# Output weights in three whole-row transfers, and the first chunk's output groups in two passes

## The chip, the core and the metric

The kernel runs on one core of a Trainium2 chip. The metric is the device time of one execution in microseconds. A time without a profile is the median of several runs; a profiled execution has a time of its own. In the profile PE is TensorE (PEld its weight loads), DVE is VectorE, ACT is ScalarE, POOL is GpSimd and SP is SyncE. A trailing q (SPq, POOLq) means that the engine only issues a transfer. L531 is line 531 of the kernel.

## What is computed

Cosine attention over 8 batches of 12 heads, 448 positions and 64 dimensions, then two matrix products with a leaky ReLU between them:

```python
q_n = q / (norm(q) + 1e-6);  k_n = k / (norm(k) + 1e-6)
scores = q_n @ k_n.T / 0.1
attn = exp(scores - max) / (sum + 1e-9)
x = (attn @ v).transpose(0, 2, 1, 3).reshape(3584, 768)
h = x @ w_in                        # 768 x 2048
out = maximum(0.01 * h, h) @ w_out  # 2048 x 768, result float32
```

## The kernel before

**Attention.** Heads are handled in pairs: slot s is one pair, or one half of a pair of pairs from slot 12 on, 48 slots in all. Each slot goes through a row of steps, each a small function. `load_qk(s)` reads float32 rows on SP's queue (L150 from slot 12 on, L158 to L161 before). `squares(s)` runs on POOL (L216, L224), `sums(s)` adds them up on DVE (L232, L238), `roots(s)` takes logarithm and exponential on ACT (L245, L246), and `normalise(s)` multiplies on DVE (L253, L254, then L260 or L270, which writes `qn`). `transposes(s)` is done by PE below slot 12 (L284) with a copy out of PSUM by DVE (L325); from slot 12 on it is a DVE transpose (L306), and for odd slots six transfers on SP's queue carry the result into `qkT` (L315). `scores` is PE work (L346) followed by exponentials on ACT (L355). `attend(j)` makes the row sums and the products with v on PE (L366), the reciprocal on ACT (L377, L378) and the scaling on DVE (L397), which writes `xT`, the input of the first product. `settle(s)` is normalise, transposes (from slot 12 on), `hold` and the squares of slot s + 2. `hold` (L616, POOL) and `hold_loads` (L613, SP) are tiny operations that read `qn`, so that what is queued behind them on their engine starts no sooner.

**The two products.** The 3584 tokens go in eight chunks of 384 or 512. `first(c, m)` makes one of 16 row blocks of the hidden layer for chunk c: PE (L494) and an activation on ACT (L505) into `hT`. `second(c, ts, half)` makes 128 tokens by 384 output columns: 16 matmuls, one for each row block m (L531), a copy by DVE from PSUM into `osb` (L541), and after the second half a store on SP's queue (L548). Chunk 0 makes all three `ts` of the left half and then all three of the right half; the others make both halves of a `ts` in turn.

**Order.** The program order on each engine is written out by hand up to slot 15. There `feed_groups(0, n)` puts the next n pieces of chunk 0's work between attention steps. A planner spreads the later chunks over 42 visits, and chunk 7 comes last.

**PSUM.** There are eight banks. `banks(1)` or `banks(2)` deals out the bank, or the aligned pair, that was dealt longest ago. PE's next use of a bank waits until ACT or DVE has read out what was there before.

**Weights.** `w_in` comes in four transfers on POOL's queue (L104), `w_out` in two (L110): each brings half of the columns of all 16 row blocks, casting float32 to bf16, so one contiguous piece is 384 columns (768 bytes as written) and a transfer has 128 x 16 of them. The first is issued in the last of the six opening slots, the second after `squares(10)` and one load of v. Loads of v (L176, L184) are on the same queue.

The code writes the hand order with s = 6, so its `s + 7` is slot 13.

Of the kernel before, what the change touches and what calls it, by code (L numbers as in the profile page):

```python
# [8 lines left out]
F32 = mybir.dt.float32  # L9
BF16 = mybir.dt.bfloat16  # L10
AF = mybir.ActivationFunctionType
ALU = mybir.AluOpType
# [4 lines left out]
def kernel(  # L17
# [10 lines left out]
    nc = tc.nc  # L28
    B, H, S, D = q.shape
    N_tok, D_model = out.shape  # L30
# [4 lines left out]
    MAIN = 3 * 128  # L35
# [5 lines left out]
    MT = D_ff // 128  # L41
# [33 lines left out]
    def banks(count, keep=None):  # L75
        lo, hi = (0, 8) if not deals["apart"] else (0, 4) if count == 2 else (4, 8)
        x = min(
            (i for i in range(lo, hi, count) if not set(range(i, i + count)) & set(kept.values())),
            key=lambda i: max(age[i : i + count]),
        )  # L80
        deals["n"] += 1
        age[x : x + count] = [deals["n"]] * count
        if keep:
            kept[keep] = x
        return ps[:, x] if count == 1 else ps[:, x : x + count]
# [19 lines left out]
            out=w_in_sb[:, e::2, n0 : n0 + D_ff // 2], in_=w_in_r[e, :, :, n0 : n0 + D_ff // 2]  # L105
        )

    def load_w_out(half):
        n0 = half * HALF
        gp.dma_start(out=w_out_sb[:, :, n0 : n0 + HALF], in_=w_out_r[:, :, n0 : n0 + HALF])  # L110

    def main(x, b, h0, nh):
        return x[b, h0 : h0 + nh, 0:MAIN].rearrange("h (p t) d -> p h t d", t=3)
# [57 lines left out]
    def load_v(j):  # L171
        if j >= B * NQ:
            return
        b, jj = divmod(j, NQ)
        vb[j] = vbp.tile([128, 4, 3, D], BF16, name="v_b")
        gp.dma_start(out=vb[j], in_=main(v, b, 4 * jj, 4))  # L176
# [32 lines left out]
    def squares(s, eng=gp, parts=(0, 1)):  # L209
        if s >= NSLOT:  # L210
            return
        sq = sqt[s % 3]
        if s >= OLD:
            sqs[s] = sq
            x = raw[s].rearrange("p (t d) -> p t d", d=D)
            gp.tensor_tensor(sq[:, :, :D], x, x, op=ALU.mult)  # L216
            return
        sqs[s] = halves(sq.rearrange("p t d -> p (t d)"), D + 1)
        for i in parts:
            x, y = raw[s][i], sqs[s][i]  # L220
            if eng is nc.scalar:
                nc.scalar.activation(y[..., :D], x, func=AF.Square)
            else:
                eng.tensor_tensor(y[..., :D], x, x, op=ALU.mult)  # L224

    def sums(s, parts=(0, 1)):
        if s >= NSLOT:
            return
        if s not in ss:
            ss[s] = smp.tile([128, 14], F32, name="ss")  # L230
        if s >= OLD:
            nc.vector.tensor_reduce(  # L232
                ss[s], sqs[s], axis=AX.X, op=ALU.add
            )
            return
        for i in parts:
            o = ss[s][:, 0:8] if i == 0 else ss[s][:, 8:14]
            nc.vector.tensor_reduce(  # L238
                o.rearrange("p (h t) -> p h t", h=2), sqs[s][i], axis=AX.X, op=ALU.add
            )  # L240
# [239 lines left out]
    def chunk_cols(c):  # L480
        return (0, MAIN) if c % 2 == 0 else (MAIN, 512)
# [41 lines left out]
    def second(c, ts, half):  # L523
        c0, n = chunk_cols(c)
        last = c == B - 1 and ts == n // 128 - 1
        pieces = ((0, HALF // 2), (HALF // 2, HALF)) if last and half == 1 else ((0, HALF),)
        x, end = c0 + ts * 128, c0 + (ts + 1) * 128
        for lo, hi in pieces:
            po2 = banks(1)
            for m in range(MT):  # L530
                nc.tensor.matmul(  # L531
                    out=po2[:, : hi - lo],
                    lhsT=hT[c][:, m, ts * 128 : (ts + 1) * 128],
                    rhs=w_out_sb[:, m, half * HALF + lo : half * HALF + hi],
                    start=(m == 0), stop=(m == MT - 1),
                )
            if half == 0 or last:
                osb[c, ts] = osp.tile([128, D_model], F32, name="osb")
            o = osb[c, ts]
            cols = slice(half * HALF + lo, half * HALF + hi)  # L540
            nc.vector.tensor_copy(out=o[:, cols], in_=po2[:, : hi - lo])  # L541
            if half == 1 or last:
                if not last:
                    cols = slice(0, D_model)
                row = 0
                while row < 128:
                    dst, cnt = rows_of(c, x + row, end)
                    nc.sync.dma_start(out=dst[:, cols], in_=o[row : row + cnt, cols])  # L548
                    row += cnt


    work = {}
    for c in range(B):
        c0, n = chunk_cols(c)
        groups = [(KT * n, lambda c=c, m=m: first(c, m)) for m in range(MT)]
        order = [(ts, half) for half in range(2) for ts in range(n // 128)] if c == 0 else [
            (ts, half) for ts in range(n // 128) for half in range(2)
        ]
        work[c] = groups + [
            (MT * HALF, lambda c=c, ts=ts, half=half: second(c, ts, half)) for ts, half in order  # L560
        ]

    def feed_groups(c, count):
        for _ in range(count):
            work[c].pop(0)[1]()
# [49 lines left out]
    def hold(x):  # L615
        gp.tensor_copy(out=seen, in_=x)  # L616
# [35 lines left out]
    for s in range(NPAIR):  # L652
        j = s // 2 - 1 if s >= 2 else None
        even = s % 2 == 0
        n = s + 2 if 0 < s < NPAIR - 2 else None
        last = s == NPAIR - 1
        if not last:
            scores(s, (0,))
        scores(s, (1,))
        if j is not None and not even:  # L660
            products(j, 1)
        if j is not None and even:
            totals(j)
        elif not last:
            fill(2)
        if n and s > 1:
            sums(n, (0,))
        if not last:
            normalise(s + 1)
        if s < 2:  # L670
            sums(s + 2, (0, 1) if s == 0 else (0,))
        if s == 0:
            load_qk(7)
        elif s in (2, 3):
            hold_loads(s + 1)
            load_qk(s + 6)
        if s == 3:
            sums(n, (1,))
        if late:
            scale(late.pop(), 1)  # L680
        if j is not None and not even:
            scale(j, 0)
        if last:
            scale(j, 1)
            sums(NPAIR)
            sums(NPAIR + 1)
            load_w_out(0)
        else:
            hold(qn[s + 1][:, 6, 0, 0:1])
        squares(s + 3)  # L690
        if s == 0:
            load_v_rem(0, range(2, 4))
        if s in (1, 2):
            load_v(s)
        if last:
            load_v(NQ)
            load_v_rem(1)
        elif s < 2:
            load_w_in(s)
        elif s > 2:  # L700
            load_w_in(s - 1)
        if n and even:
            sums(n, (1,))
        scores(s, (2,))
        if last:
            for m in range(2):
                first(0, m, (0, 2))
            scores(s, (3,))
            for kt in (1, 3):
                for m in range(2):  # L710
                    first(0, m, (kt,))
        elif not even:
            fill(2)
            if s == 3:
                roots(n)
            transposes(s + 1)
            scores(s, (3,))
            if s == 1:
                sums(n, (1,))
                roots(n)  # L720
            fill(2)
        elif s == 0:
            roots(2)
            transposes(1)
            fill(2)
        else:
            transposes(s + 1)
            products(j, 0)
            if s == NPAIR - 2:
                scores(s + 1, (0,))  # L730
            if n:
                roots(n)
        if j is not None and not even and not last:
            late.append(j)
# [39 lines left out]
    hold(qn[s + 2][:, 6, 0, 0:1])  # L774
    squares(s + 4)
    load_v(s // 2 + 1)
    load_w_out(1)
    sums(s + 3)
    feed_groups(0, 2)
    scores(s + 1, (0, 1))  # L780
# [12 lines left out]
    normalise(s + 4)  # L793
    hold(qn[s + 4][:, 6, 0, 0:1])
    squares(s + 5)
    load_v(s // 2 + 2)
    hold_loads(s + 4)
    load_qk(s + 7)
# [6 lines left out]
    def settle(s, more=()):  # L805
        normalise(s)
        if s >= OLD:
            transposes(s)
        hold(qn[s][:, 6, 0, 0:1])
        for x in (*more, s + 2):  # L810
            squares(x)
# [9 lines left out]
    settle(s + 5, (s + 6,))  # L821
    hold_loads(s + 5)
    load_qk(s + 8)
    feed_groups(0, 1)
    sums(s + 6)
    transposes(s + 5)
    attend(NQ)
# [3 lines left out]
    scores(s + 3, (3,))  # L831
    load_qk(s + 9)
    settle(s + 6)
    sums(s + 7)
    feed_groups(0, 1)
    roots(s + 7)

    scores(s + 4, (2,))
    scores(s + 5, (0, 1))
    feed_groups(0, 1)  # L840
    attend(NQ + 1)
    load_qk(s + 10)
    settle(s + 7)
    sums(s + 8)

    scores(s + 5, (2, 3))
    feed_groups(0, 1)
    load_vq(0)
    roots(s + 8)
    load_qk(s + 11)  # L850
    settle(s + 8)
    load_qk(s + 12)
    sums(s + 9)
    feed_groups(0, 1)
    roots(s + 9)
    attend(NEWQ - 1)
    feed_groups(0, 1)

# [131 lines left out]
```

## Time and profile before

| | |
|---|---|
| median of three runs | 417.78 us (417.63 to 418.49) |
| profiled execution | 416.43 us |
| its span in the trace | 414.6 us |
| PE busy | 407.1 us, 98% of the span |
| DVE, ACT, POOL busy | 221.5, 250.2, 114.6 us |
| granted PE clock | 1.00 in every stretch |
| first and second `w_out` transfer | issued at 29.11 and 49.12 us, landed 23.2 and 21.3 us later |
| chunk 0's output groups on PE | between 55.00 and 80.89 us |
| DMA packets of POOL's queue, q0 | 15488, 11.80 MB |

The profiled execution's time is 1.83 us more than its span. Times in the trace count from the start of the span. A row of the timeline gives start, duration, engine, line, operation, and in brackets idle time before it with what ended it. The DMA rows give, for a queue and a stretch, its packets, megabytes and the time that its packets took as a share of 16 DMA engines; shares of the two queues can add up to more than 100%, because packets in flight overlap.

### The profile page before, as it was taken

How to read it: one execution, taken by the hardware profiler on the slowest of the kernel's cores; microseconds unless marked ns; L12 is line 12 of the kernel's file. 1: busy time of each engine (PE TensorE's matmuls, PEld its weight loads, DVE VectorE, ACT ScalarE, POOL GpSimd, SP SyncE). 2: the span in 40 equal slices, each digit the busy share in tenths (PEclk: the TensorE clock that was granted, in tenths of full speed). 3: DMA queues.
4: the chain of work that ended last, by engine and by line, in shares of the span. 5: the costliest groups of instructions: out<-in, count | busy, mean ns of one | idle time of the engine just before them, and what ended most of it. 6: DMA issues, size and time to landing. Idle time of an engine off the chain costs nothing.

```text
span 414.6 us, 11342 instructions
## 1 busy us (share of the span) xinstructions
PE 407.1 (98%) x4799; PEld 212.3 (51%) x4799; DVE 221.5 (53%) x387; ACT 250.2 (60%) x431; POOL 114.6 (28%) x149
## 2 busy tenths in 40 slices
PE   8899999999999999999999999999999999999997
PEld 3335555544555555544455555554445555654565
DVE  6977976855778556766474964464621301210022
ACT  5997876378657785668865688547764464004300
POOL 4875543433234132413331433122210000000000
PEclk9999999999999999999999999999999999999999
DMA  7999998775377851884275681742442100020022
GB/s 195 242 214 220 210 234 187 181 223 129 60 206 182 204 132 22 204 229 99 53 186 157 151 229 43 175 126 84 91 90 68 51 39 3 38 77 0 2 76 76
DMA packets 41964, 53.82 MB, mean 130 GB/s; under 512 B 12474, under 2 KB 32314, under 8 KB 41914
## 3 DMA queue, kind: packets, MB, share of 16 engines
q1 hardware_dynamic: 25738, 41.01, 35.0%
q0 software_dynamic: 15488, 11.80, 19.7%
q8 instruction: 37, 0.61, 0.6%
q10 hardware_dynamic: 688, 0.30, 0.2%
q14 instruction: 13, 0.11, 0.1%
HBM read 45.61 MB, written 11.01 MB: 137 GB/s over the span
## 4 chain that ended last, share of the span: by engine, by line
PE 87%; DMA 4%; ACT 3%; DVE 3%; POOL 2%; SPq 1%; issue 1%; POOLq 0%
PE ps L531 34%; PE ps L494 34%; PE ps L442 9%; PE ps L417 7%; ACT pe L355 2%; DMA qk_h<-in_k_dram 2%; PE ps L366 2%; DVE qn L270 1%; DMA xT<-in_k_dram 1%; DMA xT<-in_q_dram 1%; POOL sq L224 1%; PE ps L346 1%; POOL sq L216 1%; DVE ss L238 0%; SPq L131 0%
## 5 line engine op out<-in xcount | busy, mean ns | idle before, releaser
L531 PE MATMUL ps<-w_out_sb,hT 128*128 128x384 bf16 (+1 forms) x912 | 151.3, 324 | 0.3 <-DVE xT L397 0.3
L494 PE MATMUL ps<-xT,w_in_sb 128*128 128x384 bf16 (+1 forms) x768 | 151.1, 353 | 0.0
L423 ACT ACTIVATE pe<-ps 128x896 bf16<-128x896 f32 x126 | 108.9, 915 | 46.1 <-PE ps L417 46.1
L531 PEld LDWEIGHTS <-hT 128*128 128x128 bf16 x912 | 86.5, 98 | 64.3 <-issue 10.0
L494 PEld LDWEIGHTS <-w_in_sb 128*128 128x128 bf16 x768 | 72.6, 98 | 74.3 <-issue 9.7
L505 ACT ACTIVATE hT<-ps 128x384 bf16<-128x384 f32 (+1 forms) x128 | 67.4, 552 | 56.0 <-PE ps L494 55.0
L541 DVE COPY osb<-ps 128x384 f32<-128x384 f32 (+1 forms) x57 | 31.2, 548 | 100.7 <-PE ps L531 100.6
L216 POOL TENSOR_TENSOR sq<-qk_h 128x896 f32<-128x896 f32 x36 | 61.0, 1695 | 9.2 <-DMA qk_h<-in_k_dram 7.7
L616 POOL CAST seen<-qn 128x1 f32<-128x1 bf16 x46 | 8.5, 185 | 169.4 <-DVE qn L260 160.5
L260 DVE TENSOR_TENSOR qn<-qk_h,r 128x896 bf16<-128x896 f32 x36 | 42.4, 1176 | 1.2
L232 DVE TENSOR_REDUCE ss<-sq 128x14 f32<-128x910 f32 x36 | 38.0, 1054 | 1.1 <-POOL sq L216 1.1
L355 ACT ACTIVATE pe<-ps 128x896 bf16<-128x896 f32 x42 | 35.9, 917 | 1.8 <-PE ps L346 1.7
L417 PE MATMUL ps<-qkT 64*32 64x448 bf16 x1008 | 36.5, 353 | 0.0
L253 DVE TENSOR_REDUCE r<-norms 128x14 f32<-128x28 f32 x48 | 8.6, 178 | 48.3 <-ACT norms L246 47.7
L467 DVE TENSOR_TENSOR xT<-ps,rb 128x448 bf16<-128x448 f32 x32 | 18.4, 617 | 23.2 <-PE ps L442 21.5
L306 DVE STREAM_TRANSPOSE tt<-qn 128x448 f32<-128x448 f32 x36 | 29.6, 821 | 0.9
L442 PE MATMUL ps<-pe,vq 64*32 64x448 bf16 x1008 | 27.0, 349 | 0.0
L245 ACT ACTIVATE ss<-ss 128x14 f32<-128x14 f32 x48 | 10.3, 214 | 25.4 <-DVE ss L232 24.4
L417 PEld LDWEIGHTS <-qkT 64*32 64x32 bf16 x1008 | 13.1, 91 | 19.2 <-issue 14.5
L442 PEld LDWEIGHTS <-vq 64*32 64x32 bf16 x1008 | 14.5, 92 | 8.0 <-issue 0.3
L442 PE MATMUL ps<-pe,ones 64*32 64x448 bf16 x560 | 15.1, 349 | 0.0
L346 PE MATMUL ps<-qkT 64*64 64x448 bf16 (+1 forms) x132 | 12.9, 359 | 2.1 <-ACT pe L355 1.2
(53 smaller groups left out, 218.9 us busy)
## 6 DMA issues: line engine op xcount, KB each, us to landing
qk_h<-in_q_dram SPq DMA_DIRECT2D x36, 224.0 KB, 4.0
qk_h<-in_k_dram SPq DMA_DIRECT2D x36, 224.0 KB, 4.3
out_dram<-osb SPq DMA_DIRECT2D x20, 384.0 KB, 2.3
qkT<-tt SPq DMA_DIRECT2D x72, 56.0 KB, 3.3
qkT<-tt SPq DMA_DIRECT2D x36, 112.0 KB, 3.5
vq<-in_v_dram POOLq DMA_DIRECT2D x16, 224.0 KB, 5.0
w_in_sb<-in_moe_w_in_dram POOLq DMA_DIRECT2D x4, 768.0 KB, 11.2
w_out_sb<-in_moe_w_out_dram POOLq DMA_DIRECT2D x2, 1536.0 KB, 22.3
```

The costliest lines, as they stand in the source:

```text
L216: gp.tensor_tensor(sq[:, :, :D], x, x, op=ALU.mult)
L232: nc.vector.tensor_reduce(ss[s], sqs[s], axis=AX.X, op=ALU.add)
L260: nc.vector.tensor_tensor(qn[s].rearrange("p m d e -> p m e d"), raw[s].rearrange(f"p ({t[1:-1]} d) -> p m e d", e=n, d=D), r.rearrange(f" ...
L306: nc.vector.transpose(out=to.rearrange(("p g (c m) -> p m g c", "p g (m c) -> p m g c")[which], m=7), in_=qn[s].bitcast(F32).rearrange("p ...
L355: nc.scalar.activation(out=dst, in_=sc[:, :, :S], func=AF.Exp, scale=inv_tau)
L417: nc.tensor.matmul(out=sc[32 * strip : 32 * strip + 32, a, :S], lhsT=x[rows, c0 : c0 + 32], rhs=x[rows, 0:S], start=True, stop=True,)
L423: nc.scalar.activation(out=pq[u, i], in_=sc[:, :, :S], func=AF.Exp, scale=inv_tau)
L442: nc.tensor.matmul(out=po[32 * strip : 32 * strip + 32, w, :S], lhsT=weights, rhs=pq[us[x if two else 0], i][rows, a, :], start=(i == 0), ...
L494: nc.tensor.matmul(out=pm[:, :n], lhsT=w_in_sb[:, kt, m * 128 : (m + 1) * 128], rhs=xT[c // 2][:, kt, c0 : c0 + n], start=(done + i == 0), ...
L505: nc.scalar.activation(out=hT[c][:, m, :n], in_=pm[:, :n], func=AF.Prelu, alpha=0.01)
L531: nc.tensor.matmul(out=po2[:, : hi - lo], lhsT=hT[c][:, m, ts * 128 : (ts + 1) * 128], rhs=w_out_sb[:, m, half * HALF + lo : half * HALF + ...
L541: nc.vector.tensor_copy(out=o[:, cols], in_=po2[:, : hi - lo])
```

## The change

`w_out` is loaded by whole rows of 768 columns instead of half rows: row blocks 0 to 7 where the first half was loaded, blocks 8 to 11 where the second half was, and blocks 12 to 15 after `squares(11)`, ahead of the load of v there. Chunk 0's six output groups of 16 matmuls become twelve of eight matmuls: pass 0 over row blocks 0 to 7 for each `ts` and half, copied into `osb`; pass 1 over blocks 8 to 15, added by DVE to `osb` in float32, with the store after the right half. From slot 11 on, each feed of one group becomes a feed of two. The feed near slot 12 now comes ahead of `sums(13)` and `roots(13)`. `normalise(13)`, `transposes(13)`, `load_qk(16)`, `hold` and `squares(15)` move ahead of a feed and `attend(4)`. The planner's part is as it was.

```diff
-    def load_w_out(half):
-        n0 = half * HALF
-        gp.dma_start(out=w_out_sb[:, :, n0 : n0 + HALF], in_=w_out_r[:, :, n0 : n0 + HALF])
+    def load_w_out(lo, hi):
+        gp.dma_start(out=w_out_sb[:, lo:hi], in_=w_out_r[:, lo:hi])
...
+    def second_of_two(ts, half, part):
+        c0, n = chunk_cols(0)
+        x, end = c0 + ts * 128, c0 + (ts + 1) * 128
+        po2 = banks(1)
+        ms = range(part * MT // 2, (part + 1) * MT // 2)
+        cols = slice(half * HALF, (half + 1) * HALF)
+        for m in ms:
+            nc.tensor.matmul(
+                out=po2[:, :HALF],
+                lhsT=hT[0][:, m, ts * 128 : (ts + 1) * 128],
+                rhs=w_out_sb[:, m, cols],
+                start=(m == ms[0]), stop=(m == ms[-1]),
+            )
+        if part == 0:
+            if half == 0:
+                osb[0, ts] = osp.tile([128, D_model], F32, name="osb")
+            nc.vector.tensor_copy(out=osb[0, ts][:, cols], in_=po2[:, :HALF])
+            return
+        o = osb[0, ts]
+        nc.vector.tensor_tensor(o[:, cols], o[:, cols], po2[:, :HALF], op=ALU.add)
+        if half == 1:
+            dst, cnt = rows_of(0, x, end)
+            assert cnt == 128
+            nc.sync.dma_start(out=dst, in_=o)
...
+    work[0][MT:] = [
+        (MT * HALF // 2, lambda ts=ts, half=half, part=part: second_of_two(ts, half, part))
+        for part in range(2) for ts in range(MAIN // 128) for half in range(2)
+    ]
...
-            load_w_out(0)
+            load_w_out(0, 8)
...
-    load_w_out(1)
+    load_w_out(8, 12)
...
     squares(s + 5)
+    load_w_out(12, 16)
     load_v(s // 2 + 2)
...
     load_qk(s + 8)
-    feed_groups(0, 1)
+    feed_groups(0, 2)
     sums(s + 6)
...
     settle(s + 6)
+    feed_groups(0, 2)
     sums(s + 7)
-    feed_groups(0, 1)
     roots(s + 7)
 
     scores(s + 4, (2,))
     scores(s + 5, (0, 1))
-    feed_groups(0, 1)
+    normalise(s + 7)
+    transposes(s + 7)
+    load_qk(s + 10)
+    hold(qn[s + 7][:, 6, 0, 0:1])
+    squares(s + 9)
+    feed_groups(0, 2)
     attend(NQ + 1)
-    load_qk(s + 10)
-    settle(s + 7)
     sums(s + 8)
 
     scores(s + 5, (2, 3))
-    feed_groups(0, 1)
+    feed_groups(0, 2)
...
-    feed_groups(0, 1)
+    feed_groups(0, 2)
     roots(s + 9)
     attend(NEWQ - 1)
-    feed_groups(0, 1)
+    feed_groups(0, 2)
```

More of the change, by code (lines that the diff above doesn't have):

```diff
@@ L555 @@
         groups = [(KT * n, lambda c=c, m=m: first(c, m)) for m in range(MT)]
-        order = [(ts, half) for half in range(2) for ts in range(n // 128)] if c == 0 else [
-            (ts, half) for ts in range(n // 128) for half in range(2)
-        ]
-        work[c] = groups + [
-            (MT * HALF, lambda c=c, ts=ts, half=half: second(c, ts, half)) for ts, half in order
-        ]
+        work[c] = groups + [
+            (MT * HALF, lambda c=c, ts=ts, half=half: second(c, ts, half))
+            for ts in range(n // 128) for half in range(2)
+        ]
+    work[0][MT:] = [
+        (MT * HALF // 2, lambda ts=ts, half=half, part=part: second_of_two(ts, half, part))
+        for part in range(2) for ts in range(MAIN // 128) for half in range(2)
+    ]
     def feed_groups(c, count):
```

## The prediction

> **What bounds the kernel now.** I read the page first, then PE's waits, PE's busy time by stretches, and, around the change, the timeline and the DMA rows.
>
> ```profile
> PE 407.1 (98%) x4799; PEld 212.3 (51%) x4799; DVE 221.5 (53%) x387; ACT 250.2 (60%) x431; POOL 114.6 (28%) x149
> ```
>
> PE is idle for 414.6 - 407.1 = 7.5 us. By the stretches 3.67 us lie before 20 us and 2.89 us behind the last matmuls; the change touches neither. What is left is 0.47 us (25 to 30 us), 0.25 us (at 48.83) and 0.26 us (at 70.49), together 0.98 us: all that better timing can win. 0.2% is 0.83 us, about what a measurement of this kernel can tell from no change. The last two gaps lie where the change works:
>
> ```profile
> 48.83 0.34 PE L284 MATMUL ps<-id,qn 128*128 128x128 bf16 x3 [0.25 <-DVE qn L270]
> 70.49 5.38 PE L531 MATMUL ps<-w_out_sb,hT 128*128 128x384 bf16 x32 [0.26 <-DVE xT L397]
> PEld L531 <- DMA w_out_sb<-in_moe_w_out_dram: 0.7, 1, 0.7
> ```
>
> The second row names DVE, but by the order of deals that group uses bank 7, read out by 67.9 us (the copy at 67.38 + 0.56). The third row, from PEld's waits, names the real one: the second weight transfer landed at 49.12 + 21.3 = 70.4 us.
>
> The stage before that lives off slot 10:
>
> ```profile
> 46.09 2.27 POOL L224 TENSOR_TENSOR sq<-qk_h 128x512 f32<-128x512 f32 x2 [1.76 <-DMA qk_h<-in_k_dram]
> 46.25 2.52 DVE L270 TENSOR_TENSOR qn<-qk_h,r 128x512 bf16<-128x512 f32 x2
> 48.70 1.15 DVE L238 TENSOR_REDUCE ss<-sq 128x8 f32<-128x520 f32 x2
> 49.77 0.61 DVE L325 COPY qkT<-ps 128x896 bf16<-128x896 bf16 x1
> 50.87 1.16 DVE L270 TENSOR_TENSOR qn<-qk_h,r 128x512 bf16<-128x512 f32 x2
> 51.76 0.67 PE L284 MATMUL ps<-id,qn 128*128 128x128 bf16 x7
> ```
>
> POOL waits for slot 10's load until 46.09; squares, sums, roots and normalise follow, and PE transposes at 51.76, while `qn` is still being written (50.87 + 1.16 = 52.03). There is no slack: a later load of slot 10 shows on PE. While POOL squares, DVE's pair of L270 takes 2.52 us against 1.16 elsewhere; that makes the 0.25 us gap.
>
> That load shares the DMA engines with the weights. Two stretches, 34 to 36 us (`w_in`, 2048-byte packets) and 40 to 44 us (`w_out`, 768 bytes):
>
> ```profile
> q0 software_dynamic: 186, 0.35, 92.6%
> q1 hardware_dynamic: 167, 0.08, 19.6%
> ```
>
> ```profile
> q0 software_dynamic: 668, 0.52, 81.7%
> q1 hardware_dynamic: 666, 0.36, 42.7%
> ```
>
> q0 is POOL's queue, q1 is SP's. With both backlogged they alternate about packet by packet (668 to 666), whatever the size; so q1 got 0.04 MB/us beside large packets and 0.09 beside small ones.
>
> **The change part by part.** *PE work.* The 96 matmuls stay, at the same places (16 at each feed); 32 in a row take 5.38 us against 2 x 2.7, so a change of group costs nothing. Pass 0 needs only `hT` 0 to 7, which frees nothing: PE is busy until 55.00. Zero.
>
> *Packets of the first transfer.* 1024 of 1536 bytes instead of 2048 of 768. One takes 0.817 x 64 us / 668 = 78 ns at 768 bytes and 0.926 x 32 us / 186 = 159 ns at 1881 bytes; between them 134 ns at 1536, an estimate from these two rows. One q0 packet in its turn came every 16 x 4 / 668 = 96 ns per engine; it becomes about 145 ns. From 40 us on, slot 10 still lacked about 680 of q1's packets (1510 moved from 40 to 50 us, of which slot 11 has 832, with the completion packets): 680 x 96 / 16 = 4.1 us before, 680 x 145 / 16 = 6.2 us after. Slot 10 lands 2.1 us later. Bounds: none (if turns went by bytes) and 4 us (q1 got only 39 packets in the microsecond from 37 to 38, pure `w_in`); I take 2.1 us, from the rows on either side of 1536 bytes. Then squares run from 48.2 to 50.0 (1.82 us), the second sum ends at 50.6 against 49.85, and the copy of slot 9's `qkT`, behind the sums on DVE, at 51.15 against 50.38. It frees the bank of `first(0, 13)`, which started at 50.77; and `qn` of slot 10 ends 0.75 us later. The collision that made the 0.25 us gap is gone, since slot 9 is normalised before the squares start. PE's shift: **+0.8 us** (0 to +2.6).
>
> *POOL's queue.* Issuing took 1.16 us for 2048 packets, 0.82 for 512 (the load of v): 0.94 + 0.82 + 0.82 instead of 2 x 1.17. The middle piece is issued after slot 10's squares, about 51 us instead of 49.12, the last one about 55.5. POOL's next squares wait for `hold` on `qn` of slots 10 and 11 anyway. Zero in itself.
>
> *The wait for weights.* The second half of the bytes costs 1024 x 134 / 16 = 8.6 us of all engines instead of 2048 x 78 / 16 = 10, and takes a larger share against q1. From 55.5 us with half of it left it lands by about 66, before PE wants it at 71 or later. **-0.26 us**.
>
> *Slot 13's load.* It was issued at 54.33 and took until 62.53, POOL's squares waiting. The last piece now goes beside it in larger packets, but there is less in front. Bounds for its landing: -3 us (the page's median for such loads is 4.3 us, here it took 7.3 to 7.5) and +5 us (loads beside `w_in` took up to 12.7). I take +1: half of it went beside `w_out` before, too. `sums(13)` can take 0.6 us of it without harm, as it has to wait for two copies now (below). **+0.4 us** (0 to +3).
>
> *DVE and the banks.* Six more evacuations, 12 instead of 6; the copy takes 0.55 us, the add is bounded by that and by L397's 0.617 for 448 columns: 3.4 us more, in a stretch (56 to 81 us) where DVE is idle for 6.4 us. The path is through the banks. Replaying the deals, `ts` 1 of pass 0 gets banks 6 and 7, and `ts` 2 gets 6 and 7 again, with three score tiles between; before, one feed took one bank. The copy out of bank 6 lies behind slot 12's normalise and transpose on DVE (63.22 + 1.00): it ends at about 64.8, and PE wants the bank at 64.57: 0.25 us. The second copy ends at 65.3, and only then `sums(13)` starts, 0.6 us later than at 64.72; `roots(13)` stands on ACT ahead of the exponentials of slots 10 and 11, so the first of these ends at 67.8 instead of 67.15. `totals(4)`, which took bank 6, now takes bank 2 from that exponential, when PE comes at 67.5: 0.25 us. **+0.5 us** (0 to 1).
>
> *The moved steps.* Slot 13's `tt` comes some 4 us sooner (before at 72.57, after `attend`'s scaling); its six transfers were issued from 73.37 over 3.77 us and landed about 3.4 us later, at 80.5, for use at 80.89. That thin cover grows. `load_qk(16)`, issued at 63.26, now stands behind them, about 73, and lands at 77; `squares(16)` ran at 76.67 and `sums(16)` at 83.71. Nothing on the path. `osb` holds three tiles at a time, as before. From 81 us on PE waits for nothing, and replaying the planner's deals with the new ages shows no new conflict.
>
> Sum: 0.8 - 0.26 + 0.4 + 0.5 = +1.4 us. The profiled execution would go from 416.43 to 417.9; it lies 1.35 us below the median of the runs, and the runs from 417.78 to **419.2 us**.
>
> **The rules that speak to it.** The Trainium skill, DMA: Bandwidth & Descriptors, section SWDGE vs HWDGE vs iDMA, says that a DMA engine changes context only at the border of a packet of preferably up to 4096 bytes and at most 64 descriptors. By that rule a turn would hold about the same bytes before and after, q1 would lose nothing, and the first rival below would hold. The even counts beside packets of two sizes speak against it.
>
> The same page, section Rules for kernel authors, asks for one large transfer in place of several, and its section Anatomy of one DMA gives some 2 us fixed for each. No row here separates that part; with it the last piece would land 2 us later, by estimate at 68.
>
> **The rivals.** *Only the banks count (0.24).* If turns go by bytes, slots 10 and 13 land as before: +0.5 - 0.26 = +0.25 us, 418.0 us, no difference that shows. For it: the stretches beside large packets may have had less waiting on q1. Against: slot 10 was on its way then.
>
> *Faster (0.10).* Fewer packets move the same bytes in 8.6 instead of 10 us per half. If q1 keeps its rate, its loads come sooner once POOL's queue is empty, at 48 instead of 51 us. Place: slots 10 to 13; price: both gaps (0.51 us), perhaps part of the 0.47 us and of stalls shorter than a matmul, which the modelled ends hide: -0.5 to -1 us, 417.0 us. It decides if slot 10 lands before 46.0 us and the banks cost under 0.2 us. Against: that slot's packets stand in turns with the first transfer's.
>
> *The last piece is late (0.11).* It is issued 6 us later than those bytes were. If q0 moves bytes no faster than before, it lands at 72.5; PE comes at 71.5 and waits 1 us more, with the banks' 0.5: 419.0 to 419.6 us. Against: the queue's order and its bytes are the same, and its packets are cheaper.
>
> **How the numbers follow.** The forecast has 0.55. Its own range is 418.3 to 421.5 (slot 10 by 1 to 3.5 us, slot 13 up to 2 us). Taking in the banks-only case and part of the faster one gives 417.3 to 421.8. Slower: 0.52 of the forecast, 0.09 of the late piece, 0.01 of the banks-only case: 0.62. Faster 0.08 (the case's less harmful part is within the bound). Within: 0.30.
>
> **What would show it.** q0's packets fall by 2048 - 16 to 13456. The first transfer's flight falls from 23.2 to about 20 us. POOL's squares of slot 10 start near 48.2; PE has a gap of about 1 us near 51 for DVE, none for `w_out` at 71, and gaps of 0.2 to 0.3 us near 64.6 and 67.5. Chunk 0's last group ends near 82.4 instead of 80.9, and the rest follows unchanged. The prediction is wrong if slot 10's squares start at 46, if PE's idle time after 20 us falls, or if time is lost behind 81 us.

## The result, and the profile after

The changed kernel takes 418.54 us (median of 22 runs, 417.63 to 419.14) where the kernel before takes 417.20 us (22 runs): +1.34 us between the medians, ratio 1.0029 (95% interval 1.0020 to 1.0037). It is slower by about 0.3%. Its profiled execution took 418.08 us with a span of 416.0 us, against 416.43 and 414.6: +1.4 us of span.

The page's engine row and, from its DMA queues, POOL's queue:

```profile
PE 405.9 (98%) x4783; PEld 212.4 (51%) x4799; DVE 222.4 (53%) x393; ACT 250.3 (60%) x431; POOL 113.8 (27%) x150
q0 software_dynamic: 13456, 11.80, 19.0%
```

There are six more DVE instructions, 2032 fewer packets, and the same bytes. (Of PE's 4799 matmuls 16 have no record in this trace; so its busy time is not compared here, but the starts of its groups.) PE's timeline before, at the places to compare:

```profile
50.77 1.15 PE L494 MATMUL ps<-xT,w_in_sb 128*128 128x384 bf16 x6
55.00 2.77 PE L531 MATMUL ps<-w_out_sb,hT 128*128 128x384 bf16 x16
80.89 0.76 PE L417 MATMUL ps<-qkT 64*32 64x448 bf16 x24
```

And after:

```profile
48.31 0.55 PE L283 MATMUL ps<-id,qn 128*128 128x128 bf16 x7
51.73 1.14 PE L493 MATMUL ps<-xT,w_in_sb 128*128 128x384 bf16 x6 [1.20 <-DVE qkT L324]
52.92 0.81 PE L283 MATMUL ps<-id,qn 128*128 128x128 bf16 x7
56.30 2.77 PE L558 MATMUL ps<-w_out_sb,hT 128*128 128x384 bf16 x16
66.18 2.76 PE L558 MATMUL ps<-w_out_sb,hT 128*128 128x384 bf16 x16 [0.24 <-DVE osb L567]
71.88 5.38 PE L558 MATMUL ps<-w_out_sb,hT 128*128 128x384 bf16 x32
82.27 0.76 PE L416 MATMUL ps<-qkT 64*32 64x448 bf16 x24
```

The seven transposes at 48.31 run without the 0.25 us gap of before. Then PE waits 1.20 us for a `qkT` copy, which reads out the bank that `first(0, 13)` is to use. The gap at 66.18 is new. The group at 71.88 has no gap, and PEld's waits no longer name `w_out`. The planner's first scores start, and so chunk 0's output groups end, at 82.27 instead of 80.89: +1.38 us, all of the span's difference; the rest follows unchanged.

POOL and DVE show where the 1.20 us come from:

```profile
48.73 1.83 POOL L223 TENSOR_TENSOR sq<-qk_h 128x512 f32<-128x512 f32 x2 [4.67 <-DMA behind<-qn]
49.80 1.34 DVE L237 TENSOR_REDUCE ss<-sq 128x8 f32<-128x520 f32 x2 [2.28 <-POOL sq L223]
51.06 0.61 DVE L324 COPY qkT<-ps 128x896 bf16<-128x896 bf16 x1
52.17 1.16 DVE L269 TENSOR_TENSOR qn<-qk_h,r 128x512 bf16<-128x512 f32 x2
```

The squares of slot 10 start at 48.73 instead of 46.09, and DVE, which had no gap there, waits 2.28 us. POOL's row names the tiny `behind` transfer, issued after slot 10's load on the same queue; the chain of waits names the load itself, from its issue on:

```profile
36.25 12.32 DMA qk_h<-in_k_dram
```

It was in flight for 12.3 us; before, it was issued at 36.38 and the squares began at 46.09. The two DMA queues from 40 to 44 us and from 44 to 48 us:

```profile
q0 software_dynamic: 402, 0.62, 84.2%
q1 hardware_dynamic: 403, 0.29, 29.5%
```

```profile
q0 software_dynamic: 429, 0.66, 90.1%
q1 hardware_dynamic: 430, 0.18, 24.8%
```

Again the two queues move one packet for one. From 44 to 48 us before the change it was:

```profile
q0 software_dynamic: 641, 0.49, 78.3%
q1 hardware_dynamic: 645, 0.39, 43.9%
```

SP's queue moved 833 packets in these 8 us instead of 1311 (666 + 645).

### The profile page after: what moved, and what is told of

Read it like the earlier page. It is cut to its first block, busy times and chain, and to the rows that moved or that the text cites. A ratio compares the mean times of both kernels' runs of the same rounds, so it can differ in the third digit from the quotient of the medians.

```text
span 416.0 us, 11334 instructions
## 1 busy us (share of the span) xinstructions
PE 405.9 (98%) x4783; PEld 212.4 (51%) x4799; DVE 222.4 (53%) x393; ACT 250.3 (60%) x431; POOL 113.8 (27%) x150
## 3 DMA queue, kind: packets, MB, share of 16 engines
q0 software_dynamic: 13456, 11.80, 19.0%
## 4 chain that ended last, share of the span: by engine, by line
PE 86%; DVE 4%; DMA 4%; ACT 3%; issue 1%; SPq 1%; POOL 0%; POOLq 0%; DVEq 0%
PE ps L493 32%; PE ps L530 32%; PE ps L441 9%; PE ps L416 7%; PE ps L558 3%; DMA qk_h<-in_k_dram 3%; ACT pe L354 2%; PE ps L365 2%; DVE qn L269 1%; DVE ss L237 1%; PE ps L345 1%; DMA xT<-in_q_dram 1%; DVE qkT L324 0%; DVE qn L259 0%; SPq L130 0%
## 5 line engine op out<-in xcount | busy, mean ns | idle before, releaser
L530 PE MATMUL ps<-w_out_sb,hT 128*128 128x384 bf16 (+1 forms) x816 | 134.9, 323 | 0.0
L530 PEld LDWEIGHTS <-hT 128*128 128x128 bf16 x816 | 77.5, 98 | 56.6 <-issue 8.5
L540 DVE COPY osb<-ps 128x384 f32<-128x384 f32 (+1 forms) x51 | 27.9, 547 | 99.1 <-PE ps L530 99.0
L252 DVE TENSOR_REDUCE r<-norms 128x14 f32<-128x28 f32 x48 | 8.6, 179 | 48.8 <-ACT norms L245 48.3
L558 PE MATMUL ps<-w_out_sb,hT 128*128 128x384 bf16 x96 | 16.5, 326 | 0.2 <-DVE osb L567 0.2
```

What stands on the lines that cost most here:

```text
L530: nc.tensor.matmul(out=po2[:, : hi - lo], lhsT=hT[c][:, m, ts * 128 : (ts + 1) * 128], rhs=w_out_sb[:, m, half * HALF + lo : half * HALF + ...
L558: nc.tensor.matmul(out=po2[:, :HALF], lhsT=hT[0][:, m, ts * 128 : (ts + 1) * 128], rhs=w_out_sb[:, m, cols], start=(m == ms[0]), stop=(m = ...
```

## The experiments

Theory A: large packets on POOL's queue make the turns longer, and slot 10's load lands late. Rival B: the two passes cost the time, through their evacuations, banks and moved steps. Each kernel was compared with the kernel before on the same chip. Where PE's stage is given, it runs from the start of the first output group to that of the four groups (two pairs before the change) fed ahead of `attend(5)`: 15.49 us before (55.00 to 70.49), 15.58 after (56.30 to 71.88).

**Small packets again, in the changed kernel.**

```diff
-        gp.dma_start(out=w_out_sb[:, lo:hi], in_=w_out_r[:, lo:hi])
+        w = D_model if lo else HALF
+        for n0 in range(0, D_model, w):
+            gp.dma_start(
+                out=w_out_sb[:, lo:hi, n0 : n0 + w], in_=w_out_r[:, lo:hi, n0 : n0 + w]
+            )
```

> The changed kernel, with row blocks 0 to 7 of w_out loaded as two transfers of 384 columns each (768-byte packets, 2048 in all), everything else as changed. Theory A (larger packets of POOL's queue take longer turns, so slot 10's load lands late): slot 10's squares start near 46.1 us instead of 48.7, the 1.2 us gap of PE at 51.7 is gone and the 0.25 us gap near 48.8 is back; the time falls by about 1.2 us to +0.1 us against the kernel before, ratio 1.000. Rival B (the two passes with their extra evacuations, banks and moved steps cost the time; packet size does not matter): still 1.003.

Ratio 1.0000 (0.9989 to 1.0012), 417.67 us. POOL's timeline and the queues from 40 to 44 us:

```profile
45.90 2.27 POOL L227 TENSOR_TENSOR sq<-qk_h 128x512 f32<-128x512 f32 x2 [1.69 <-DMA qk_h<-in_k_dram]
q0 software_dynamic: 663, 0.51, 81.0%
q1 hardware_dynamic: 657, 0.37, 42.6%
```

Slot 10 is back where it was, the gap near 51 is gone, and so is the loss. The gap near 48.8, which was expected back, did not come in this trace. These are two transfers where there was one before the change, but SP's queue moves as much beside them (657 packets) as beside that one (666); so it is the size of the packets that counts, not the number of transfers. B falls as the main cause. The stage took 16.05 us in this trace (54.81 to 70.86), longer than in the changed kernel; the experiments below look for the reason.

**Whole rows without the passes.**

```diff
-    def load_w_out(half):
-        n0 = half * HALF
-        gp.dma_start(out=w_out_sb[:, :, n0 : n0 + HALF], in_=w_out_r[:, :, n0 : n0 + HALF])
+    def load_w_out(lo, hi):
+        gp.dma_start(out=w_out_sb[:, lo:hi], in_=w_out_r[:, lo:hi])
...
-                    rhs=w_out_sb[:, m, half * HALF + lo : half * HALF + hi],
+                    rhs=w_out_sb[:, m if c else m % 8, half * HALF + lo : half * HALF + hi],
...
-            load_w_out(0)
+            load_w_out(0, 8)
...
-    load_w_out(1)
+    load_w_out(8, 16)
```

> The kernel before, with only the loads changed: whole rows, blocks 0 to 7 and then 8 to 15, in the two old places. So that chunk 0's groups wait for no later piece, they multiply row blocks 0 to 7 of w_out twice instead of 0 to 15 (same work, other numbers for chunk 0). Theory A: squares of slot 10 start near 48.7, PE waits about 1.2 us for a qkT copy near 51.7, the 0.26 us wait for w_out is gone: about +0.9 us, ratio 1.002. Rival B: only the wait for w_out goes, -0.26 us, ratio 0.9994.

Ratio 1.0021 (1.0008 to 1.0035), as theory A has it. PE's timeline, in an execution 0.6 us longer than the median of this kernel:

```profile
52.63 1.14 PE L493 MATMUL ps<-xT,w_in_sb 128*128 128x384 bf16 x6 [1.91 <-DVE qkT L324]
```

The load alone makes the wait, in a kernel that has no pass; slot 10's squares began at 49.62 here. The stage took 15.16 us: this is what it takes without any wait, so the wait for `w_out` was worth 15.49 - 15.16 = 0.33 us before, and the passes cost 15.58 - 15.16 = 0.42 us, in one profiled execution each.

**The bank behind the transpose.**

```diff
-    settle(s + 6)
+    normalise(s + 6)
+    hold(qn[s + 6][:, 6, 0, 0:1])
+    squares(s + 8)
     feed_groups(0, 2)
+    transposes(s + 6)
     sums(s + 7)
```

> The changed kernel, with the DVE transpose of slot 12 moved behind the feed of ts 1 (so behind its two copies on DVE). If the 0.24 us gap of PE at 66.2 comes from bank 6, whose copy stands behind that transpose, it is gone: -0.3 us against the changed kernel, ratio 1.002. If it has another cause, nothing changes: 1.003. It says nothing on the 1.2 us gap, which both theories leave in place here.

Ratio 1.0029 (1.0019 to 1.0040): nothing gained. The gap moved:

```profile
65.90 2.77 PE L558 MATMUL ps<-w_out_sb,hT 128*128 128x384 bf16 x16
69.00 0.75 PE L365 MATMUL ps<-pe,ones 128*32 128x448 bf16 x12 [0.33 <-ACT pe L354]
```

The wait at the bank of `ts` 1 is gone, and `totals(4)` waits instead for an exponential that stands behind slot 13's sum. The same edit on top of the small packets:

> Both edits together: first piece in 768-byte packets, slot 12's transpose behind the two copies. Theory A: no gap at 51.7 and none at 66.2, no wait for w_out; the 0.25 us gap near 48.8 stays as before the change: 0 to -0.3 us against the kernel before, ratio 0.9993 to 1.000. Rival B: about 1.002.

Ratio 1.0008 (0.9999 to 1.0017), between the two theories. In the trace PE waits 0.46 us for a `qkT` copy at 61.61 and 0.79 us at `totals(4)`, and slot 12's multiplication on DVE takes 2.22 us beside slot 13's squares, instead of 1.17; the stage took 17.1 us.

**Slot 13's sum ahead of slot 12's transpose.** The edit is the one above, with the lines `sums(s + 7)` and `transposes(s + 6)` exchanged.

> The changed kernel, with slot 12's DVE transpose moved behind the two copies of ts 1 and behind slot 13's sum. With the transpose behind the copies alone, the wait for bank 6 at 66.2 gave way to a wait of totals(4) at 69.0 for an exponential that stands behind roots(13). If these two waits are one backlog on DVE, both go now: -0.3 us against the changed kernel, ratio 1.002 to the kernel before, and no gap of PE between 60 and 71 us. If the cost of the two passes lies elsewhere: 1.003. The gap near 51.7 stays.

In the trace both waits are gone and the stage takes 15.33 us (56.55 to 71.88) instead of 15.58. But slot 10's load came later in this profile (squares at 48.98), and the ratio is 1.0036 (1.0023 to 1.0049), 418.9 us over five runs: the runs don't show the expected 0.3 us, and 1.002 lies outside the interval. The two waits are one backlog on DVE by the trace; their price of 0.25 us is the trace's alone.

> The same edit, and the first piece in 768-byte packets as in the first experiment. Theory A and one backlog on DVE: of the gaps between 30 and 80 us only the 0.25 us near 48.8 stays; 0.3 us less than the kernel before, ratio 0.9993. If removing one wait only uncovers the next, as it did before: 1.000 to 1.001.

Ratio 1.0010 (1.0002 to 1.0019), the stage 16.14 us: with slot 10 in time, something else costs 1 us. DVE and POOL:

```profile
67.11 2.13 DVE L263 TENSOR_TENSOR qn<-qk_h,r 128x896 bf16<-128x896 f32 x1
66.51 1.68 POOL L219 TENSOR_TENSOR sq<-qk_h 128x896 f32<-128x896 f32 x1 [1.65 <-DMA qk_h<-in_q_dram]
```

Slot 13's multiplication runs beside slot 14's squares and takes 2.13 us; in the changed kernel it begins at 68.61, as the squares end (66.89 + 1.68 = 68.57), and takes 1.18. Behind it on DVE stand the two copies of `ts` 2 that free the bank of the last scores, where PE waits (0.32 us at 70.41, for `osb`).

**The collision taken away.**

```diff
     hold(qn[s + 6][:, 6, 0, 0:1])
-    squares(s + 8)
     feed_groups(0, 2)
     sums(s + 7)
...
     hold(qn[s + 7][:, 6, 0, 0:1])
+    squares(s + 8)
     squares(s + 9)
```

> The kernel with the first piece in 768-byte packets and slot 13's sum ahead of slot 12's transpose, and in addition slot 14's squares on POOL moved behind the normalising of slot 13 on DVE. There the two ran together and the multiplication of slot 13 took 2.13 us instead of 1.17. If that collision holds back the copies behind it, and they hold back PE's bank for scores at 70.4: the multiplication takes 1.2 us, the stage from the first output group to the fourth pair falls from 16.1 to about 15.2 us, and the time is 0.3 us under the kernel before, ratio 0.999 to 1.000. If the 0.9 us comes from elsewhere: 1.001 as before.

Ratio 0.9990 (0.9979 to 1.0001), 416.99 us. The multiplication took 1.19 us. In the profiled execution another wait, 0.45 us for a `qkT` copy at 61.60, kept the stage at 16.0 us instead of the expected 15.2; the wait at the bank of the last scores is gone. A second series of this kernel:

> The kernel with the first piece in 768-byte packets, slot 13's sum ahead of slot 12's transpose and slot 14's squares behind slot 13's normalising, once more, to see whether it is faster than the kernel before. If the three costs found are all that the two passes have, and the wait for w_out is gone: 0.9985 to 0.9995, the interval with the first series below 1. If its first series was luck: 1.000.

0.9992 (0.9982 to 1.0001), 417.02 us; here the stage took 15.19 us and no wait at a bank is left:

```profile
67.17 1.19 DVE L263 TENSOR_TENSOR qn<-qk_h,r 128x896 bf16<-128x896 f32 x1
70.31 5.37 PE L562 MATMUL ps<-w_out_sb,hT 128*128 128x384 bf16 x32
80.71 0.76 PE L420 MATMUL ps<-qkT 64*32 64x448 bf16 x24
```

Chunk 0 ends at 80.71 us, 0.18 us sooner than before the change. Taken together, weighting each series by its interval, that is 0.9991 (about 0.9984 to 0.9998): this version may be 0.1% faster than the kernel before. It isn't shown: neither series shows it alone, and the kernel chosen for a second series was the one whose first had come out best.

**The steps not moved.** Slot 13's normalise, transpose and load back behind `attend(4)`, first in the kernel with small packets and the sum first, then in the changed kernel:

```diff
-    normalise(s + 7)
-    transposes(s + 7)
-    load_qk(s + 10)
-    hold(qn[s + 7][:, 6, 0, 0:1])
-    squares(s + 9)
     feed_groups(0, 2)
     attend(NQ + 1)
+    load_qk(s + 10)
+    settle(s + 7)
     sums(s + 8)
```

> The same kernel with slot 14's squares where they were, and slot 13's normalise, transpose and load back behind attend(4), as before the change. The collision goes in another way: about 15.2 us for that stage, no wait for w_out, ratio 0.999 to 1.000. If the two passes cost time by themselves, and not by where the steps stand: 1.001.

Ratio 1.0011 (1.0000 to 1.0023). The stage took 15.16 us, as expected, but the ratio is that of the other theory, since the gain is given back behind the stage: PE stops within the planner's first scores (at 82.53) for DVE's scaling, as in the next kernel.

> The changed kernel with only the moved steps of slot 13 back behind attend(4), large packets as changed. In the changed kernel the normalising of slot 13 started just as slot 14's squares had ended (1.18 us, no collision), so the move cost nothing there: 1.003 as in the changed kernel, or up to 0.2 us less through the bank of the last scores. If the move is part of the change's cost: 1.001 to 1.002.

Ratio 1.0053 (1.0040 to 1.0066), a clear miss: a kernel 1 us slower than the changed one (419.59 us). PE's timeline:

```profile
66.26 2.76 PE L558 MATMUL ps<-w_out_sb,hT 128*128 128x384 bf16 x16 [0.89 <-DVE osb L567]
82.35 0.73 PE L416 MATMUL ps<-qkT 64*32 64x448 bf16 x9
83.27 0.84 PE L416 MATMUL ps<-qkT 64*32 64x448 bf16 x15 [0.19 <-DVE xT L396]
```

The first 24 score matmuls took 1.76 us from start to end (82.35 to 84.11) instead of 0.76. The two scalings of `attend(5)`, which free the bank that PE waits for, ran from 82.06 instead of 80.30: on ACT the reciprocal stands behind `roots(15)`, and slot 15's sum came at 79.44 instead of 77.69, since on DVE slots 13 and 14 had come later. The wait at 66.26 grew from 0.24 to 0.89 us because slot 12's multiplication met slot 13's squares (2.06 us). The edited lines stand behind that place, so the edit doesn't explain it; and as PE had come there 0.57 us sooner than in the changed kernel, it was only 0.08 us later at the start of these scores (82.35 against 82.27). So the move is no part of the cost; it saves some 1 us that the two passes cost without it, as these scores ended at 84.11 instead of 83.03.

**The first piece in two parts, and in quarter rows.** Both are built on kernels above: on the one with the sum first, blocks 0 to 3 at the old place and `load_w_out(4, 8)` ahead of the load of v behind slot 10's squares; on the one with small packets, pieces of 192 columns.

> The changed kernel with slot 13's sum ahead of slot 12's transpose, and the first piece cut in time: row blocks 0 to 3 at the old place, 4 to 7 after slot 10's squares, both in 1536-byte packets. Theory A: only 512 large packets stand in turns with slot 10's load, so its squares start at 45 to 46.5 us and the gap at 51.7 is gone; blocks 4 to 7 are issued near 48.5 and take 5 to 8 us, so PE may wait for them at 55: 0.9995 with no such wait, up to 1.004 with 2 us of it. Rival B: 1.002 to 1.003 in any case.

Ratio 1.0081 (1.0049 to 1.0113). The runs lie far apart, from 417.71 to 424.18 us, and the profiled execution is the longest of them, with a granted clock of 0.991; so its waits are not those of a typical run. In it the load of slot 10 was in flight for 10.7 us, between 9.7 and 12.3: half as many large packets cost 0.4 times as much. Its squares began at 48.34, not by 46.5 as was expected, the load having been issued 1.2 us later than in the changed kernel. PE waited for the later blocks:

```profile
60.88 4.00 PE L558 MATMUL ps<-w_out_sb,hT 128*128 128x384 bf16 x12 [3.88 <-DMA w_out_sb<-in_moe_w_out_dram]
```

> The changed kernel with the first piece as four transfers of 192 columns: 4096 packets of 384 bytes. A third point for theory A: if q0 and q1 take turns packet by packet, one q0 packet per engine comes about every 70 ns instead of 96 or 145, and slot 10's squares start near 45 us, before the 46.0 of the 768-byte packets; but 4096 turns last until about 56, so that PE waits for the weights near 55. If packet size does not matter to slot 10's load: it lands as in the changed kernel, near 48.7.

One run, 419.86 us, beside 417.33. The landing can't be read: issuing the four transfers took POOL 3.5 us, its later issues of v had to wait for transfers, and slot 9's squares ran only at 47.02. The rate can, from 40 to 44 us and from 44 to 48 us:

```profile
q0 software_dynamic: 927, 0.41, 77.3%
q1 hardware_dynamic: 839, 0.46, 53.9%
```

```profile
q0 software_dynamic: 1022, 0.39, 78.3%
q1 hardware_dynamic: 860, 0.46, 56.0%
```

In these 8 us SP's queue moved 833 packets beside packets of 1536 bytes, 1311 beside 768 (before), and 839 + 860 = 1699 beside 384. That is the third point for A, with one difference: POOL's queue moved more than SP's here. The counts are even only in some of the microseconds (213 to 217 from 41 to 42, 215 to 220 from 45 to 46); whether SP's queue had less waiting in the others isn't shown.

## Why the prediction was right

Forecast: slower by 1.4 us, 419.2. Measured: +1.34 us between the medians, in the range and on the side that had 0.62. (Both medians came 0.6 us lower than the three runs from which the forecast started.) Term by term, from the starts of PE's groups:

- *PE's own work, the places of the feeds, the stretch behind 81 us*: nothing, as forecast. POOL's packets came out at 13456, as worked out.
- *Packets of the first transfer*: +0.8 forecast, about +1.2 measured (PE's lag is +0.12 us at 40 us and +1.30 at 56). The mechanism held; the size of a turn was the term that was off: 16 x 4 / 402 = 159 and 16 x 4 / 429 = 149 ns, not 145. (The prediction's two rows, 96 ns at 768 bytes and 16 x 2 / 186 = 172 ns at 1881, give 148 at 1536.) Its 680 packets were through at 44.1 us before and, by q1's counts of each microsecond, at 46.6 after: 2.5 us later, not 2.1, so the squares began at 48.73, not 48.2. The first transfer was in flight for 22.0 us, not the 20 that were forecast.
- *The wait for weights*: -0.26 forecast, -0.32 measured (PE's lag falls from +1.71 to +1.39 us at this group).
- *Slot 13's load*: +0.4 forecast, nothing measured. This is the step that failed: its two transfers took 6.4 and 7.3 us (7.1 and 7.5 before), not a microsecond more, and its squares began sooner (62.01 instead of 62.53). The likely reason, which no run tests, is that fewer bytes were in front. The last piece itself landed at 55.38 + 12.6 = 68.0 us, not by 66, but PE came for it only at 71.88.
- *Banks*: +0.5 forecast, +0.4 measured. The wait of `ts` 2 for bank 6 came at 0.24 us where 0.25 was forecast. The one at `totals(4)` did not show: PE came at 68.94, as the first of those exponentials, begun at 67.99 and some 0.9 us long, had just ended. It appeared at 0.33 us as soon as the first was taken away.
- *Moved steps*: nothing lost, as forecast. But the cover that was named, the landing of slot 13's `qkT`, is not what they were seen to give: without them PE waited for the scaling of `attend(5)`, and the kernel was a microsecond slower. The prediction also gave no price to what slot 13's multiplication, moved forward, would run beside. In the changed kernel that cost nothing by luck, as it began just when slot 14's squares had ended; with slot 10 in time the two met.

The sum was nearer than its terms, and that is luck: the first was too small by what slot 13 was too large.

The rule that a DMA engine changes context only at the border of a packet of preferably up to 4096 bytes (the Trainium skill, DMA: Bandwidth & Descriptors, section SWDGE vs HWDGE vs iDMA) would have left slot 10 alone. The trace does not agree: 402 to 403 and 663 to 657, records of 1536 and of 768 bytes, one for one. In this kernel the two queues share by records of the trace, not by 4096 bytes; how many records go in one turn the counts don't show.

## What to carry to other kernels

Longer contiguous pieces made this bulk load cheaper (22.0 us in flight instead of 23.2), and the other queue slower while it ran: work out the rate of the small loads that share the engines, and look for the one with no slack. A gap on PE that is removed may only uncover the next one in the same backlog, so price the stage (start of one group to start of another) and not the gap. Ask of every step that a change moves what it will run beside.

## What was not expected of the hardware

The prediction saw at slot 10 that DVE's multiplication and POOL's squares stretch each other, and did not look for it at slots 12 to 14. In these traces the multiplication of two SBUF operands and the squares exclude each other: alone the multiplication takes 1.17 us and the squares 1.68. In the kernel with small packets the squares began at 66.18, the multiplication at 66.92, and it ended at 68.90, which is 1.04 us after the squares' end at 67.86; without the passes, 64.01, 64.23 and 66.71, which is 1.02 us after. Before the change POOL came second:

```profile
62.02 1.17 DVE L260 TENSOR_TENSOR qn<-qk_h,r 128x896 bf16<-128x896 f32 x1
62.53 2.16 POOL L216 TENSOR_TENSOR sq<-qk_h 128x896 f32<-128x896 f32 x1 [3.64 <-DMA qk_h<-in_k_dram]
```

The squares took 2.16 us and ended 1.50 us after the multiplication. Whichever comes second seems to wait until the first is done. The Trainium skill, SBUF — State Buffer, section Who interferes with whom, says that the port pair that DVE and GpSimd share is an exclusive lock, that a DVE instruction with two SBUF inputs contends for it with a GpSimd instruction that reads SBUF, and that the order of issue decides who blocks; these traces agree. In the changed kernel PE and DVE, late by slot 10's load, came past the collision of slot 13's multiplication with slot 14's squares (68.61 against 68.57), so that cost and relief came from one delay.
